# A gated decode layer on one core: first MLP layer as 16 wide products, first half of the output projection in whole 448-column rows, fewer and wider idle matmuls

## The chip, the cores and the metric

The kernel runs on one core of one Trainium2 chip. The metric is the device time of one execution in microseconds; the number for the kernel before is the median of five runs.

## The reference

One decode step of a layer with two branches, for a batch of 8 rows of width 448. Branch A is attention over a window of 1024 cached positions (16 query heads, 8 key/value heads, head size 256), followed by an output projection. Branch B is a two-layer MLP on the normalised input. A sigmoid gate g mixes the two.

```python
W = min(4096, max(256, Sk // 4))                 # 1024 of 4096 positions
q = (x @ wq).reshape(B, Sq, Hq, Dh)              # 8 x 1 x 16 x 256
k = jnp.repeat(k_cache[:, :, Sk - W:, :], 2, axis=1)
v = jnp.repeat(v_cache[:, :, Sk - W:, :], 2, axis=1)
p = softmax(einsum("bhqd,bhkd->bhqk", q, k) * Dh ** -0.5)
a = einsum("bhqk,bhkd->bhqd", p, v).reshape(B, Sq, 4096) @ wo      # 4096 x 448
h = gelu(layernorm(x) @ w1 + b1)                 # 448 x 1792, tanh form
b = h @ w2 + b2                                  # 1792 x 448
g = sigmoid((x * gate_w).sum(-1, keepdims=True))
return g * a + (1 - g) * b
```

## The kernel before

All large inputs pass once through a ring of nine slots of 2 MB each (`slots`, filled by `pump`). The order of the loads is written out by hand in `plan`: `wq` in two slots, the keys of step 0, `w1`, `w2`, then keys and values of the 16 steps in turn (values two steps behind the keys, `LAG`), and last `wo` in two slots. The first `wo` slot holds quarters 0 and 1 of the projection and comes as one transfer; the second holds quarters 2 and 3 and comes as three (quarter 2, six eighths of quarter 3, the last two eighths). SyncE's queue issues each load when `done()` has freed a slot. The order of work on each engine is the order in which the program writes it (`manual_schedule`).

A step u handles four key/value heads of one batch row. VectorE turns the keys in 32x32 blocks, in two halves (`turn_keys`, L350). TensorE multiplies them with the query weights `qw` (`scores`, L416 and L422; 8 products of 512 columns and a mask product for each half). Then come the maximum (`top`, `share`), the exponential on ScalarE (`expo`, L451), another turn on VectorE (`turn`, L464), its sum and inverse (`total`, `invert`), 16 products with the values (`values`, L494), a merge of two halves (L503, `gather` L509) and `finish` (L524, L527), which writes the scaled head outputs to `oT`. The main loop runs u = 1 to 15 and works off the parts of the steps before between the two halves of the scores.

Around the main loop:

- `norm_and_gate` and `query` prepare the normalised input `yT`, the gate `gg` and the query weights `qw`. GpSimd clears several tiles at the start.
- `mlp_hidden` (L540, L549) computes the first MLP layer transposed: 56 products whose stationary side is a 128x128 piece of `w1` and whose moving side is the 8 columns of `yT`. VectorE adds the bias and computes the GELU with ScalarE's Tanh. `mlp_out` (L585, L592) does the second layer in 14 products of 448 columns and one for the bias, and leaves the gated result in `mixb` (L594).
- `keep_clock` (L598) issues matmuls whose result nobody reads. They stand in the loop for u = 12, 13, 14 (six each) and at seven places of the tail.
- The tail, after the loop, finishes steps 14 and 15 and does the output projection. `begin` (L638) seeds two accumulators with `mixb` through an identity product: `A_lo` holds columns 0 to 223 in PSUM rows 0 to 7, `A_hi` columns 224 to 447 in rows 32 to 39. `spread_rows` (L651, L658) rearranges `oT` to `oP` by 16 small products and a VectorE copy, once for quarters 0 and 1 and once for quarters 2 and 3. `project(q)` (L667) then does eight pairs of 224-column products into the two accumulators. VectorE and ScalarE copy them to `res` (L709, L710), and one transfer stores it (L711).

Of the kernel before, what the change touches and what calls it, by code (L numbers as in the profile page):

```python
# [18 lines left out]
def kernel(  # L19
# [82 lines left out]
    def done(n=1):  # L102
        consumed[0] += n
        pump()
# [72 lines left out]
    def slot(*key):  # L177
        return slots[index[key]]

    consts.tile([P, 64], BF16, name="pad")  # L180
    x_sb = consts.tile([NB, D], BF16)
    eps_t = consts.tile([NB, 1], F32)
    rstd = consts.tile([NB, 1], F32)
# [24 lines left out]
    yz = consts.tile([NB, DT], BF16)  # L208
    nc.gpsimd.memset(xz[:], 0.0)
    xT = consts.tile([P, NX, NB], BF16)  # L210
    yT = consts.tile([P, NR + 1, NB], BF16)
    rowden = consts.tile([P, P], F32)
    sel2 = consts.tile([P, RQ], F32)
    own = consts.tile([P, PAIR], F32)
# [9 lines left out]
    each = consts.tile([NB, NB + P], F32)  # L224
    gg_s = consts.tile([P, NB], F32)
    ident_f = consts.tile([NB, NB], F32)
    ones_r = consts.tile([1, NB], BF16)
    mixb = consts.tile([NB, D], F32)
    res = consts.tile([NB, D], BF16)
    nc.gpsimd.tensor_copy(ident_f[:], ident[0:NB, 0:NB])  # L230
    nc.gpsimd.memset(ones_r[:], 1.0)

    def transposed(dst, src, srcz):
        tp = ps_misc.tile([P, NX, NB], BF16, tag="misc", name="tp")
# [56 lines left out]
    def norm_and_gate():  # L291
        stats = consts.tile([NB, nc.vector.BN_STATS_DIM], F32)
        nc.vector.bn_stats(stats[:], x_sb[:])
        mv = consts.tile([NB, nc.vector.BN_AGGR_DIM], F32)
        nc.vector.bn_aggr(mv[:], stats[:])
        nc.scalar.activation(rstd[:], mv[:, 1:2], ACT.Sqrt, bias=eps_t[:], scale=1.0)
        nc.vector.reciprocal(rstd[:], rstd[:])
        y_sb = consts.tile([NB, D], BF16)
        nc.vector.tensor_scalar(
            y_sb[:],  # L300
            x_sb[:],
            scalar1=mv[:, 0:1],
            scalar2=rstd[:],
            op0=ALU.subtract,
            op1=ALU.mult,
        )
        nc.vector.tensor_copy(
            yz[:].rearrange("p (b c r) -> p b c r", b=2, c=8),
            y_sb[:, DM:D].rearrange("p (b r c) -> p b c r", b=2, c=8),
        )  # L310
        tp = ps_misc.tile([P, NX, NB], BF16, tag="misc", name="tp")
        for r in range(NR):
            nc.tensor.transpose(tp[:, r, :], y_sb[:, r:DM:NR], ident[:NB, :NB])
        nc.tensor.transpose(tp[0:DT, NR, :], yz[:], ident[:NB, :NB])
        nc.vector.tensor_copy(yT[:, 0:NR, :], tp[:, 0:NR, :])
        nc.vector.tensor_copy(yT[0:DT, NR, :], tp[0:DT, NR, :])
        prod = consts.tile([NB, D], F32)
        gl = consts.tile([NB, 1], F32)
        nc.vector.scalar_tensor_tensor(
            prod[:],  # L320
            in0=x_sb[:],
            scalar=1.0,
            in1=gw_b[:],
            op0=ALU.mult,
            op1=ALU.mult,
            accum_out=gl[:],
        )
        gth = consts.tile([NB, 1], F32)
        nc.scalar.activation(gth[:], gl[:], ACT.Tanh, scale=0.5)
        nc.vector.tensor_scalar(  # L330
            gg[:, 0:1], gth[:], 0.5, 0.5, op0=ALU.mult, op1=ALU.add
        )
        nc.vector.tensor_scalar(
            gg[:, 1:2], gth[:], -0.5, 0.5, op0=ALU.mult, op1=ALU.add
        )
        nc.gpsimd.memset(each[:], 1.0)
        nc.vector.tensor_scalar_mul(each[:, 0:NB], ident[0:NB, 0:NB], gg[:, 0:1])
        gp = ps_misc.tile([P, NB], F32, tag="misc", name="gp")
        nc.tensor.matmul(  # L339
            gp[:], lhsT=each[:, NB : NB + P], rhs=each[:, 0:NB], start=True, stop=True  # L340
        )
        nc.vector.tensor_copy(gg_s[:], gp[:])
# [189 lines left out]
        )  # L532

    def mlp_hidden():
        hT = ps_misc.tile([P, NF, NB], F32, tag="misc", name="hT")
        w = slot("w1")
        for r in range(NR):
            o = r * F
            for c in range(NF):
                nc.tensor.matmul(  # L540
                    hT[:, c, :],
                    lhsT=w[:, o + c : o + F : NF],
                    rhs=yT[:, r, :],
                    start=(r == 0 and c == 0),
                    stop=False,
                    skip_group_check=True,
                )
        for c in range(NF):
            nc.tensor.matmul(  # L549
                hT[:, c, :],  # L550
                lhsT=w[0:DT, NR * F + c : (NR + 1) * F : NF],
                rhs=yT[0:DT, NR, :],
                start=False,
                stop=True,
                skip_group_check=True,
            )
        done()
        z = consts.tile([P, NF, NB], F32)
        nc.vector.tensor_tensor(
            z[:],  # L560
            hT[:],
            b1_sb[:].rearrange("p (c o) -> p c o", o=1).to_broadcast([P, NF, NB]),
            op=ALU.add,
        )
        z2 = consts.tile([P, NF, NB], F32)
        nc.vector.tensor_tensor(z2[:], z[:], z[:], op=ALU.mult)
        uu = z2
        nc.vector.tensor_scalar(
            uu[:], z2[:], 0.044715, 1.0, op0=ALU.mult, op1=ALU.add
        )  # L570
        w_ = consts.tile([P, NF, NB], F32)
        nc.vector.tensor_tensor(w_[:], uu[:], z[:], op=ALU.mult)
        th = consts.tile([P, NF, NB], F32)
        nc.scalar.activation(th[:], w_[:], ACT.Tanh, scale=0.7978845608028654)
        hh = th
        nc.vector.tensor_scalar(hh[:], th[:], 1.0, 0.5, op0=ALU.add, op1=ALU.mult)
        hs = consts.tile([P, NF, NB], BF16)
        nc.vector.tensor_tensor(hs[:], hh[:], z[:], op=ALU.mult)
        return hs

    def mlp_out(hs):
        bb = ps_misc.tile([NB, D], F32, tag="misc", name="bb")
        w = slot("w2")
        for c in range(NF):
            nc.tensor.matmul(  # L585
                bb[:],
                lhsT=hs[:, c, :],
                rhs=w[:, c * D : (c + 1) * D],
                start=(c == 0),
                stop=False,  # L590
            )
        nc.tensor.matmul(bb[:], lhsT=ones_r[:], rhs=b2_r[:], start=False, stop=True)  # L592
        done()
        nc.scalar.activation(mixb[:], bb[:], ACT.Copy, scale=gg[:, 1:2])  # L594

    def keep_clock(dst, n):
        for _ in range(n):
            nc.tensor.matmul(dst, lhsT=foreign[:], rhs=place[:], start=True, stop=True)  # L598

# [9 lines left out]
    for u in range(1, NQ):  # L609
# [14 lines left out]
            invert(u - LAG)  # L624
        scores(u, 1)
        if NQ - 4 <= u < NQ - 1:
            keep_clock(idle[:], 6)
        expo(u - 1)
    u = NQ - 1
    A_lo = ps_misc.tile([NB, DH2], F32, tag="misc", name="A_lo")  # L630
    A_hi = ps_s.tile([P, W], F32, tag="S", name="A_hi")
    halves = (A_lo[:], A_hi[32 : 32 + NB, 0:DH2])
    oP = consts.tile([P, NJ8, NHQ, NB], BF16)
    oTv = oT[:].rearrange("p (q i) j b -> p i j q b", i=HPQ)

    def begin():
        for i, dst in enumerate(halves):
            nc.tensor.matmul(  # L638
                dst,
                lhsT=ident_f[:],  # L640
                rhs=mixb[:, i * DH2 : (i + 1) * DH2],
                start=True,
                stop=False,
                skip_group_check=True,
            )

    def spread_rows(q0, q1):
        pp = ps_sm.tile([P, HPQ, NJ, q1 - q0, NB], F32, tag="sm", name="pp")
        for i in range(HPQ):
            for m in range(HPQ):  # L650
                nc.tensor.matmul(  # L651
                    pp[32 * i : 32 * i + 32, m],
                    lhsT=ident[:, m::HPQ],
                    rhs=oTv[:, i, :, q0:q1, :],
                    start=True,
                    stop=True,
                )
        nc.vector.tensor_copy(  # L658
            oP[:, :, q0:q1, :], pp[:].rearrange("p m j q b -> p (m j) q b")
        )  # L660

    def project(q):
        w = slot("wo", q - q % 2)
        for j in range(NJ8):
            o = ((q % 2) * NJ8 + j) * D
            for i, dst in enumerate(halves):
                nc.tensor.matmul(  # L667
                    dst,
                    lhsT=oP[:, j, q, :],
                    rhs=w[:, o + i * DH2 : o + (i + 1) * DH2],  # L670
                    start=False,
                    stop=(q == NHQ - 1 and j == NJ8 - 1),
                    skip_group_check=True,
                )
# [6 lines left out]
    values(u - 1)  # L681
    top(u)
    share(u)
    keep_clock(A_hi[:, W // 2 : W], 3)
    invert(u - 1)
    expo(u)
    gather(u - 1)
# [2 lines left out]
    turn(u)  # L690
    total(u)
    invert(u)
    spread_rows(0, HALF)
    keep_clock(A_hi[:, W // 2 : W], 4)
    values(u)
    gather(u)
    keep_clock(A_hi[:, W // 2 : W], 3)
    finish(u)
    keep_clock(A_hi[:, W // 2 : W], 3)
    spread_rows(HALF, NHQ)  # L700
    keep_clock(A_hi[:, W // 2 : W], 2)
    project(0)
    project(1)
    keep_clock(A_hi[:, W // 2 : W], 3)
    project(2)
    keep_clock(A_hi[:, W // 2 : W], 2)
    project(3)

    nc.vector.tensor_copy(res[:, 0:DH2], halves[0])  # L709
# [32 lines left out]
```

## Time and profile before

| | |
|---|---|
| five runs, us | 190.59 median, 190.40 to 190.74 |
| profiled execution: its own time, us | 190.59 |
| its span, first to last instruction, us | 188.5 |
| granted TensorE clock, mean | 0.955 |
| busy in the span: PE, PEld, DVE, ACT, POOL, us | 135.7, 67.2, 126.3, 45.4, 6.4 |
| instructions: PE, PEld, DVE, ACT, POOL | 940, 940, 177, 93, 14 |
| transfers | 77.83 MB in 6316 packets, 413 GB/s mean |
| instruction queue q8 | 7 packets, 0.11 MB |

The profile is of one execution. PE is TensorE's matmul row and PEld its weight loads, which overlap; DVE is VectorE, ACT ScalarE, POOL GpSimd, SP SyncE. All times in the views are counted from the start of the span. The ends of matmuls are modelled, their starts are recorded. A float32 product appears as two loads and two matmuls.

### The profile page before, as it was taken

The numbers are of one execution on the slowest core, as the hardware profiler recorded it, in microseconds if no ns is written. First come the engines' busy times: TensorE is split into PE (matmuls) and PEld (weight loads), VectorE is DVE, ScalarE is ACT, GpSimd is POOL, SyncE is SP. The second block draws the span as 40 slices with busy tenths as digits, with TensorE's granted clock in tenths as the row PEclk, the third lists the DMA queues.
The fourth block names the chain that finished last, engine by engine and source line by source line (L and its number), as shares of the span: only waits on it lengthen the run. The fifth ranks groups of instructions, "written<-read, shape, count | busy, mean of one in ns | idle before, by whom it ended". The sixth has DMA issues, their size and how long they took to land.

```text
span 188.5 us, 2342 instructions
## 1 busy us (share of the span) xinstructions
PE 135.7 (72%) x940; PEld 67.2 (36%) x940; DVE 126.3 (67%) x177; ACT 45.4 (24%) x93; POOL 6.4 (3%) x14
## 2 busy tenths in 40 slices
PE   0027938998867578666967599848398969698993
PEld 0012823344424233422433344323143424245451
DVE  2850378989969494949494949495868677685300
ACT  3032220133140404040404021404022404035200
POOL 8400000000000000000000000000000000000000
PEclk9999999999999969996999859999789999999999
DMA  6999999999999999999999999999999999999990
GB/s 210 406 438 425 441 420 433 435 424 431 435 431 421 431 442 431 421 428 438 438 422 428 435 435 421 431 435 442 424 424 431 438 431 424 428 438 425 407 398 21
DMA packets 6316, 77.83 MB, mean 413 GB/s; under 512 B 841, under 2 KB 994, under 8 KB 1698
## 3 DMA queue, kind: packets, MB, share of 16 engines
q1 hardware_dynamic: 6128, 77.67, 96.9%
q8 instruction: 7, 0.11, 0.2%
q10 hardware_dynamic: 178, 0.02, 0.1%
q14 instruction: 3, 0.02, 0.0%
HBM read 77.68 MB, written 0.01 MB: 412 GB/s over the span
## 4 chain that ended last, share of the span: by engine, by line
DMA 78%; DVE 9%; PE 8%; ACT 2%; issue 1%; DVEq 0%; ACTq 0%; SPq 0%
DMA slot<-in_A_k_cache_dram 59%; DMA slot<-in_A_wo_dram 17%; DVE kt L350 4%; PE S L422 2%; DMA x_sb<-in_A_x_dram 2%; PE Sq L364 2%; ACT qw L405 1%; DVE qw L407 1%; DVE xz L242 1%; PE qt L379 1%; ACT qs L374 1%; PE qp L392 1%; PE PO L494 1%; PE A_lo L667 0%; PE gp L339 0%
## 5 line engine op out<-in xcount | busy, mean ns | idle before, releaser
L350 DVE STREAM_TRANSPOSE kt<-slot 128x2048 int32<-128x2048 int32 x32 | 73.7, 2306 | 30.9 <-DMA slot<-in_A_k_cache_dram 30.8
L422 PE MATMUL S<-kt,qw 128*128 128x512 bf16 x256 | 67.6, 409 | 29.1 <-DVE kt L350 28.6
L422 PEld LDWEIGHTS <-qw 128*128 128x128 bf16 x256 | 26.0, 102 | 67.2 <-issue 44.3
L527 ACT ACTIVATE oT<-fin,gg_s 128x16 bf16<-128x16 f32 x16 | 5.2, 328 | 74.2 <-PE fin L524 74.2
L451 ACT ACTIVATE E<-S,nmx 128x1024 bf16<-128x1024 f32 x16 | 22.2, 1390 | 1.9 <-DVE nmx L448 1.8
L434 DVE TENSOR_REDUCE mx<-S 128x1 f32<-128x1024 f32 x16 | 19.0, 1185 | 0.0
L494 PE MATMUL PO<-slot,ET 128*16 128x512 bf16 x256 | 17.5, 395 | 0.3 <-DMA slot<-in_A_v_cache_dram 0.3
L503 ACT ACTIVATE first<-PO,own 128x256 f32<-128x256 f32 x16 | 7.6, 473 | 27.1 <-PE PO L494 25.8
L416 PE MATMUL S<-place,foreign 128*128 128x512 bf16 x32 | 12.7, 397 | 0.1
L464 DVE STREAM_TRANSPOSE ET<-E 128x512 int32<-128x512 int32 x16 | 11.2, 698 | 2.2 <-ACT E L451 2.2
L442 PE MATMUL mz<-m,same 128*128 128x4 f32 x32 | 6.2, 265 | 5.6 <-ACT oT L527 5.5
L442 PEld LDWEIGHTS mz<-m,same 128*128 128x128 f32 x32 | 5.0, 195 | 7.5 <-ACT oT L527 6.6
L475 PEld LDWEIGHTS den<-rowsum,rowden 128*128 128x128 f32 x32 | 6.4, 205 | 3.1 <-issue 0.8
L494 PEld LDWEIGHTS <-ET 128*16 128x16 bf16 x256 | 5.1, 89 | 5.0 <-issue 1.2
L416 PEld LDWEIGHTS <-foreign 128*128 128x128 bf16 x32 | 3.2, 100 | 8.7 <-issue 6.9
L598 PE MATMUL A_hi<-place,foreign 128*128 128x512 bf16 x20 | 5.5, 381 | 0.0
L407 DVE CAST qw<-qp 32x512 bf16<-32x512 f32 x4 | 2.7, 687 | 3.4 <-ACT qw L405 3.4
L486 ACT ACTIVATE rsel<-sel,rb 128x8 f32<-128x8 f32 x16 | 4.7, 292 | 1.0 <-DVE rb L485 1.0
L475 PE MATMUL den<-rowsum,rowden 128*128 128x1 f32 x32 | 4.9, 222 | 0.0
L598 PEld LDWEIGHTS <-foreign 128*128 128x128 bf16 x38 | 3.3, 101 | 3.7 <-issue 0.8
L598 PE MATMUL idle<-place,foreign 128*128 128x512 bf16 x18 | 4.4, 378 | 0.0
L289 POOL MEMSET qw<- 128x5120 bf16 x1 | 4.4, 4354 | 0.0
(144 smaller groups left out, 95.5 us busy)
## 6 DMA issues: line engine op xcount, KB each, us to landing
slot<-in_A_k_cache_dram SPq DMA_DIRECT2D x16, 2048.0 KB, 35.2
slot<-in_A_v_cache_dram SPq DMA_DIRECT2D x16, 2048.0 KB, 36.8
slot<-in_A_wq_dram SPq DMA_DIRECT2D x1, 2048.0 KB, 7.6
slot<-in_A_wo_dram SPq DMA_DIRECT2D x1, 1792.0 KB
slot<-in_B_w_dram SPq DMA_DIRECT2D x1, 1568.0 KB
slot<-in_B_w_dram SPq DMA_DIRECT2D x1, 1344.0 KB, 11.8
slot<-in_A_wq_dram SPq DMA_DIRECT2D x1, 1024.0 KB, 9.7
slot<-in_A_wo_dram SPq DMA_DIRECT2D x1, 896.0 KB, 33.6
```

Source lines behind the costliest of these rows:

```text
L350: nc.vector.transpose(kt[:].rearrange("p c k x r -> p (c k x r)").bitcast(WORD), kn[:, hf * CH * Dh : (hf + 1) * CH * Dh].bitcast(WORD),)
L416: nc.tensor.matmul(S[u][:, cols], lhsT=foreign[:], rhs=place[:], start=True, stop=False)
L422: nc.tensor.matmul(S[u][:, cols], lhsT=qw[:, j, u, m * RQ : m * RQ + P], rhs=kt[:, :, k, :, par], start=False, stop=(k == NK - 1 and par = ...
L434: nc.vector.reduce_max(mx[:], S[u][:], axis=AXIS.X)
L442: nc.tensor.matmul(mz[:], lhsT=same[:], rhs=m4[:], start=True, stop=True)
L451: nc.scalar.activation(E[:].rearrange("p c x i -> p c i x"), S.pop(u)[:].rearrange("p (c i x) -> p c i x", i=PAIR, x=BLK), ACT.Exp, bias=n ...
L464: nc.vector.transpose(ET[:].rearrange("p c r i -> p (c r i)").bitcast(WORD), E[:].rearrange("p c x i -> p (c x i)").bitcast(WORD),)
L475: nc.tensor.matmul(den[u][:], lhsT=rowden[:], rhs=rowsum[:], start=True, stop=True)
L494: nc.tensor.matmul(PO[32 * t : 32 * t + PAIR * RQ], lhsT=ET[:, c, 0:RQ, :], rhs=vn[:, PAIR * c * Dh : PAIR * (c + 1) * Dh], start=(c < QUA ...
L503: nc.scalar.activation(first[:], PO[:, 0, :], ACT.Copy, scale=own[:, 0:1])
L527: nc.scalar.activation(oT[:, half * RQ : (half + 1) * RQ, :, b].rearrange("p h j -> p j h"), sm[:], ACT.Copy, scale=gg_s[:, b : b + 1],)
L598: nc.tensor.matmul(dst, lhsT=foreign[:], rhs=place[:], start=True, stop=True)
```

## The change

Three things are changed.

The first MLP layer turns its sides round: `yT`, padded to 32 columns, is the stationary side and 448 columns of `w1` move, in four row pieces by four column groups, 16 products. The result stands in four 32-row groups of `hP`. ScalarE copies it to SBUF with its columns reordered (`hS`), and VectorE turns the 32x32 blocks (`hB`), which gives the layout that the bias and GELU steps had. These are regrouped: two of VectorE's small steps are folded into fused ones, and the factor 0.5 of the GELU moves into the gate (-0.25, 0.25) and the bias vector of the second layer (2.0 instead of 1.0). The tile `yT` is cleared by GpSimd at the start, and the padding tile `pad` grows by 64 bytes.

The idle products change: in the loop two narrow ones (512 columns, bf16) and one wide one (512 columns, float32, `same` against `qw` read as float32) instead of six narrow; in the tail one wide, one wide, one wide, two narrow and two narrow, instead of 3, 4, 3, 3, 2, 3 and 2 narrow. They write to the tile `spare`.

The output projection: one `spread_rows` for all four quarters, after `finish(u)`. Quarters 0 and 1 go as 16 products of 448 columns into one accumulator, `whole`, which `begin` has seeded. ScalarE saves it to `mixb` (`save_whole`), and after quarter 2, which starts fresh accumulators in the two halves, an identity product adds it to them (`add_whole`). Quarter 3 follows.

```diff
-    yT = consts.tile([P, NR + 1, NB], BF16)
+    yT = consts.tile([P, NR + 1, BLK], BF16)
+    nc.gpsimd.memset(yT[:], 0.0)
...
     def mlp_hidden():
-        hT = ps_misc.tile([P, NF, NB], F32, tag="misc", name="hT")
+        FT = F // QUAD
+        hP = ps_misc.tile([P, FT], F32, tag="misc", name="hP")
         w = slot("w1")
-        for r in range(NR):
-            o = r * F
-            for c in range(NF):
+        for r in range(NR + 1):
+            rows = P if r < NR else DT
+            for t in range(QUAD):
+                o = r * F + t * FT
                 nc.tensor.matmul(
-                    hT[:, c, :],
-                    lhsT=w[:, o + c : o + F : NF],
-                    rhs=yT[:, r, :],
+                    hP[BLK * t : BLK * (t + 1), :],
+                    lhsT=yT[0:rows, r, :],
+                    rhs=w[0:rows, o : o + FT],
...
         done()
+        hS_ = epool.tile([P, W], BF16, tag="E", name="hS")
+        hS = hS_[:, 0 : 2 * FT].bitcast(F32).rearrange("p (c x) -> p c x", x=BLK)
+        nc.scalar.copy(
+            hS.rearrange("p c x -> p x c"),
+            hP[:].rearrange("p (x c) -> p x c", c=NF),
+        )
+        hB_ = epool.tile([P, W], BF16, tag="ET", name="hB")
+        hB = hB_[:, 0 : 2 * FT].bitcast(F32).rearrange("p (c x) -> p c x", x=BLK)
+        nc.vector.transpose(
+            hB_[:, 0 : 2 * FT].bitcast(WORD),
+            hS_[:, 0 : 2 * FT].bitcast(WORD),
+        )
+        hT = hB[:, :, 0:NB]
...
-    def keep_clock(dst, n):
+    def keep_clock(dst, n, wide=0):
+        for _ in range(wide):
+            rhs = qw[:, 0].rearrange("p u a -> p (u a)")[:, 0:W].bitcast(F32)
+            nc.tensor.matmul(dst, lhsT=same[:], rhs=rhs, start=True, stop=True)
         for _ in range(n):
             nc.tensor.matmul(dst, lhsT=foreign[:], rhs=place[:], start=True, stop=True)
...
         if NQ - 4 <= u < NQ - 1:
-            keep_clock(idle[:], 6)
+            keep_clock(idle[:], 2, 1)
...
+    def project_whole(q):
+        w = slot("wo", q - q % 2)
+        for j in range(NJ8):
+            o = ((q % 2) * NJ8 + j) * D
+            nc.tensor.matmul(
+                whole,
+                lhsT=oP[:, j, q, :],
+                rhs=w[:, o : o + D],
+                start=False,
+                stop=False,
+                skip_group_check=True,
+            )
+
+    def save_whole():
+        nc.scalar.copy(mixb[:], whole)
+
+    def add_whole():
         for i, dst in enumerate(halves):
             nc.tensor.matmul(
                 dst,
                 lhsT=ident_f[:],
                 rhs=mixb[:, i * DH2 : (i + 1) * DH2],
-                start=True,
+                start=False,
...
     share(u)
-    keep_clock(A_hi[:, W // 2 : W], 3)
+    keep_clock(spare[:], 0, 1)
...
     invert(u)
-    spread_rows(0, HALF)
-    keep_clock(A_hi[:, W // 2 : W], 4)
+    keep_clock(spare[:], 0, 1)
     values(u)
     gather(u)
-    keep_clock(A_hi[:, W // 2 : W], 3)
+    keep_clock(spare[:], 0, 1)
     finish(u)
-    keep_clock(A_hi[:, W // 2 : W], 3)
-    spread_rows(HALF, NHQ)
-    keep_clock(A_hi[:, W // 2 : W], 2)
-    project(0)
-    project(1)
-    keep_clock(A_hi[:, W // 2 : W], 3)
+    keep_clock(spare[:], 2)
+    spread_rows()
+    keep_clock(spare[:], 2)
...
+    project_whole(0)
+    project_whole(1)
+    save_whole()
     project(2)
-    keep_clock(A_hi[:, W // 2 : W], 2)
+    add_whole()
     project(3)
```

## The prediction

> **What bounds the kernel now.** I read the transfer table first, then the chain of waits, then the timeline and the windows of the last microseconds. The page's DMA row stands at 9 from the second slice to the last but one, at 407 to 442 GB/s: the kernel streams 77.67 MB and computes beside it. The chain that ended last says the same, and its end shows where compute can still count.
>
> ```profile
> 74.18 38.84 DMA slot<-in_A_k_cache_dram
> ...
> 151.93 32.97 DMA slot<-in_A_wo_dram
> 184.91 0.04 issue
> 184.95 0.26 PE A_lo L667
> ...
> 185.88 0.05 PE A_hi L667
> 185.93 0.37 DVE res L709
> ```
>
> Columns: start, length, what. Until 184.91 the chain is slots waiting for transfers. Only what follows the landing at 184.91 is compute: `project(3)`, the copy of the result, the store. So a gain or loss reaches the time in one of two ways: the last quarter of `wo` lands at another moment, or `project(3)` starts later than that landing. I call its start S; it is 184.95 now. The windows show how the stream runs dry (us; busy time of PE, PEld, DVE, ACT, POOL; clock; DMA share; GB/s):
>
> ```profile
> 182.00:183.00 1.00, 1.00 (x11) 0.26 (x9) 0.00 (x0) 0.00 (x0) 0.00 (x0) 1.00 0.95 385
> 183.00:184.00 1.00, 1.00 (x18) 0.71 (x18) 0.00 (x0) 0.00 (x0) 0.00 (x0) 1.00 0.69 267
> 184.00:185.00 1.00, 0.48 (x4) 0.13 (x4) 0.00 (x0) 0.00 (x0) 0.00 (x0) 1.00 0.14 52
> ```
>
> A share of 0.14 means about two of 16 transfer engines still at work: the landing waits for stragglers. The queue table of the window 181.5 to 183.2 names a cause, and the page its total:
>
> ```profile
> q1 hardware_dynamic: 156, 0.65, 93.9%
> q8 instruction: 1, 0.02, 3.2%
> ...
> q8 instruction: 7, 0.11, 0.2%
> ```
>
> One of seven 16 KB instruction packets falls here; 3.2% of 16 engines over 1.7 us is 0.87 us on one engine. The landing records of the piece that `project(3)` waits for have the last three of 16 engines at 184.02, 184.29 and 184.91. Without that packet the piece would be in at about 184.29, 0.62 us earlier.
>
> **Instructions.** The instruction packets come near 25, 55, 83, 112, 141, 163 and 182 us, when 236, 505, 758, 994, 1256, 1476 and 1825 of TensorE's 1905 recorded instructions (loads, products and some 25 waits) had started: one packet for about 265. The change removes: first MLP layer 112 to 32 (-80); idle products in the loop 36 to 24 (-12; a float32 product counts four) and in the tail 40 to 20 (-20); spreading 64 to 32; `project(0)` and `(1)` 64 to 32; `begin` 8 to 4; it adds 8 for `add_whole`. Sum -172, so 1733 are left. The smallest count per packet so far is 246 (1476 over 6), so a seventh is due between instruction 1722 (7 x 246) and 1825; the last quarter's 32 are held back by their transfer, so some 1700 at most are reached by then. The packet drops out of the end, and the others come later (the sixth near 170 us). That is worth the 0.62 us only if TensorE is ready.
>
> The Trainium skill, "Runtime: NRT & Kernel Launch", section Instruction fetch mechanics, gives blocks of 256 instructions and calls the cost of crossing one "mostly hidden"; the trace agrees on the spacing, not on the hiding at the stream's end. By that rule the packet is worth 0.
>
> **First MLP layer: 0.** Before, 56 products run from 21.83 to 24.47, and TensorE then waits for `qw` (25.77) and `kt` (28.85). Sixteen 448-column products cost between 0.76 us (four column groups at once) and 3.0 (one by one, at the 0.189 of L585: 14 in 2.81, the last 0.35); both end before 25.77. The copy on ScalarE lies between L405 (512 columns, 0.58) and L374 (1024, 1.02) and ends before 27, where VectorE arrives at 31.0. VectorE gains a transpose (L464, 512 words: 0.70) and loses two steps (0.22 each): +0.2 to +0.3. It idles 30.9 us waiting for K, and slots are asked for 35 us before they land, so nothing follows; uncovered it would be that 0.3. The GpSimd memset of `yT` (0.19, as `foreign`) moves the `qw` memset's end from 6.74 to 6.93, needed at 21. SP's issues, the one behind `w1` at 24.50 among them, move by under 2 us against those 35.
>
> **Idle products.** Six narrow ones take 1.46 us with the last one's 0.38, so 0.216 apiece: 1.29. No wide float32 one is in the trace; from `begin` (224 columns, a pass at 174.26, the next at 174.45) 512 columns in two passes are 0.87, and 0.87 + 0.43 = 1.30. No change in occupancy. In the tail the three wide ones replace 3, 4 and 3 narrow ones, up to 0.22 longer each; they stand before waits of 0.2 (rsel, 173.69), 0.3 (V, 176.25) and 0.4 us (os, 178.46), so 0 to 0.1, taken as 0.
>
> **The tail up to S.** By the landing records V of the last step is in at 176.25 and the first half of `wo` at 180.54; the change leaves both. One full spread instead of the second half: it can start at 179.6, when `oT` is ready, instead of 179.75; its copy has 256 columns (L658, 128 columns: 0.29; L509, 256 columns: 0.44 to 0.48), so `oP` is ready near 180.55. No loss. Then:
> - whole rows: 16 x 0.189 = 3.02 from 180.58, to 183.60. The halves took half of that, 16 pairs x 0.095 = 1.52, the two running side by side.
> - `project(2)`: 8 pairs x 0.095 = 0.76, to 184.36. Its piece is in at 182.73.
> - meanwhile the save: the last whole row starts at 183.42; L592 to L594 shows 0.38 from such a start to ScalarE's, so 183.80; a 448-column copy costs 0.52 (on the line through L710, 224 columns 0.34, and L405, 512 columns 0.58) to 0.62 (L594). Ready for TensorE at 184.37 to 184.47, 0.05 after its end.
> - `add_whole`: the step from 128-row products to an 8-row one leaves a gap of 0.09 (L585's last start 36.56 + 0.19, L592 at 36.84) and the step back another 0.09 (36.84 + 0.19 to 37.12). So 184.45 + 2 x 0.19 + 0.09 = 184.92. If both gaps vanish the save sets it: 184.37 + 0.38 = 184.75; if save and gaps add up, 184.47 + 0.09 + 0.38 + 0.09 = 185.03.
>
> I take 184.92, as the L592 rows are the nearest case, with ends 184.75 and 185.1. As a check: before, TensorE was ready for the last quarter at 184.37; the idle products and gaps that go took 1.50 (182.11 to 182.97, 183.73 to 184.37), the whole rows add 1.50, the add and its gaps 0.56, so it is ready at 184.93. The landing gives 0.62 back and TensorE takes it: S moves by -0.03 (-0.2 to +0.15). After S nothing changes (188.5 - 184.95 = 3.55). The profiled execution took 190.59, exactly the median, around its span of 188.5: 190.59 - 0.03, about 190.55.
>
> **Rivals.** *The landing decides (faster).* If `project(3)` is ready at 184.33, S gains 0.62: 190.0. For it: the straggler is plain, and the modelled ends of products may hide slack. Against: it needs a chain 0.6 us shorter than its own rows, of which the 3.02 is firm. It decides if `add_whole` ends by 184.3. A smaller form: if a later sixth packet changes the order of the stragglers, V and `wo` land 0.3 earlier.
>
> *The clock falls (slower).* The clock of a 3.4 us stretch follows the work of the one before:
>
> ```profile
> 62.60:66.02 3.42, 1.25 (x6) 0.42 (x5) 1.59 (x1) 0.82 (x2) 0.00 (x0) 1.00 0.97 417
> 66.02:69.43 3.41, 2.63 (x7) 0.94 (x7) 3.37 (x6) 0.00 (x0) 0.00 (x0) 0.50 1.03 442
> 120.63:124.04 3.41, 1.51 (x7) 0.57 (x6) 1.26 (x1) 1.08 (x2) 0.00 (x0) 1.00 1.04 447
> 124.04:127.46 3.42, 2.31 (x14) 1.44 (x13) 3.38 (x6) 0.00 (x0) 0.00 (x0) 1.00 0.97 417
> 160.80:164.20 3.40, 1.64 (x8) 0.68 (x7) 2.52 (x2) 0.00 (x0) 0.00 (x0) 1.00 1.05 443
> ```
>
> After 1.25 us of products it fell to 0.50, after 1.51 it stayed. At 160.8 there are 1.64, mostly idle products. If a float32 product counts half, 0.43 drops out: 1.21, below the bound. Half the clock from 164.2 makes eight scores 3.2 to 3.4 us (66.80, 28.85) instead of 1.9, and the last values, covered by 0.86 (ET done 175.46, start 176.32), come 0.6 late: 191.2. A fall in the tail itself doubles the whole rows: +3.0, 193.6. Nothing shows float32 counting less; but the covers in the tail get thinner too. The Trainium skill, "TensorE: Matmul & The Clock Gate", asks for no idle gap over about 3 us; after 150 us no gap is that long, so by it nothing falls, where the rows ask for more than 1.25 us of work.
>
> *The handover is dearer (slower).* Save, add and gaps form a serial path that is new; at 1.0 for the copy (L374) S would be 185.3: 191.0. It decides from S above 185.33.
>
> **Numbers.** No movement that counts, 0.54, its own range 190.35 to 190.75. The landing decides, 0.18, at 190.0. The clock falls, 0.20, at 191.2 and up. A dearer handover, 0.08, at 191.0. About 0.2% (0.38 us) is what a measurement of this kernel can tell from none: faster 0.18, same 0.54, slower 0.28. The range runs from the landing's 190.0 to 191.4, leaving out half of the clock's case and the better end of the first rival.
>
> **What would show it.** Right: six instruction packets, none after 175; the last `wo` pieces in before 184.5; `project(3)` starting at 184.8 to 185.1 with `add_whole`, not a transfer, as what ended its wait; clock 1.00 from 138 us on. Wrong: S set by DMA, a clock of 0.50 after 150, or a seventh packet near the end.

## The result and the profile after

The changed kernel is slower by about a third of a per cent: 191.25 us in the median of 43 executions (190.28 to 193.10) against 190.71 in 79 of the kernel before, beside it on the same chip (190.36 to 193.29). The ratio is 1.0035 with a 95% interval of 1.0022 to 1.0049. The forecast was no movement, at 190.55; the result lies inside the range, in the part kept for the slower cases.

The profiled execution took 190.91 us with a span of 189.1 (before: 190.59 and 188.5). The chain that ended last (start, length, what):

```profile
142.14 39.01 DMA slot<-in_A_wo_dram
181.20 3.10 PE A_all L673 x16
184.30 0.18 PE A_lo L701
184.87 0.28 PE A_lo L701 x3
185.15 0.28 PE A_lo L687
185.44 0.18 PE A_lo L687
185.63 0.19 PE A_lo L701
...
186.53 0.37 DVE res L744
```

Before, the last transfer on this chain was the last quarter of `wo`, and only `project(3)`, the copies and the store came behind it. Now it is an earlier one, the first half of `wo`, in at 181.15. From there on TensorE alone carries the chain: the whole rows (L673), `project(2)` (L701), the addition (L687), `project(3)` (L701). The lengths in this view are partly modelled; by the recorded starts, `project(3)` begins at 185.57, which is 0.62 later than before (184.95). The windows say the same (busy time of PE, PEld, DVE, ACT, POOL; clock; DMA share; GB/s):

```profile
183.00:184.00 1.00, 1.00 (x9) 0.43 (x7) 0.00 (x0) 0.00 (x0) 0.00 (x0) 1.00 0.65 256
184.00:185.00 1.00, 1.00 (x18) 0.70 (x14) 0.00 (x0) 0.52 (x1) 0.00 (x0) 1.00 0.12 45
185.00:186.00 1.00, 1.00 (x16) 0.52 (x16) 0.00 (x0) 0.00 (x0) 0.00 (x0) 1.00 0.00 0
```

Before, TensorE was half idle from 184 to 185, waiting for the last bytes; now it has work throughout, and the transfers are over while it still computes. The transfers themselves have changed as well. The queue table of the window 172.5 to 173.6 and the page's total:

```profile
q1 hardware_dynamic: 27, 0.44, 96.8%
q8 instruction: 1, 0.02, 5.0%
...
q8 instruction: 6, 0.10, 0.2%
```

There are six instruction packets, the sixth at 172.56. The first piece of data that lands after it, V of the last step, is in at 176.90 (before: 176.25), and the first half of `wo` at 181.15 (before: 180.54). The last quarter lands where it did, at 184.88 (before: 184.91).

### The profile page after: what moved, and what is told of

Read it like the earlier page. It is cut to its first block, busy times and chain, and to the rows that moved or that the text cites. A ratio compares the mean times of both kernels' runs of the same rounds, so it can differ in the third digit from the quotient of the medians.

```text
span 189.1 us, 2171 instructions
## 1 busy us (share of the span) xinstructions
PE 132.9 (70%) x854; PEld 63.0 (33%) x854; DVE 126.9 (67%) x175; ACT 46.8 (25%) x95; POOL 6.5 (3%) x15
## 4 chain that ended last, share of the span: by engine, by line
DMA 81%; PE 10%; DVE 5%; ACT 1%; issue 1%; SPq 0%; DVEq 0%; ACTq 0%
DMA slot<-in_A_k_cache_dram 59%; DMA slot<-in_A_wo_dram 21%; PE S L423 2%; DMA x_sb<-in_A_x_dram 2%; PE Sq L365 2%; PE A_all L673 2%; DVE xz L243 1%; DVE kt L351 1%; PE PO L495 1%; PE A_lo L701 1%; ACT qs L375 1%; PE fin L525 0%; PE qp L393 0%; PE qt L380 0%; PE mz L443 0%
## 5 line engine op out<-in xcount | busy, mean ns | idle before, releaser
L417 PEld LDWEIGHTS <-foreign 128*128 128x128 bf16 x32 | 3.2, 100 | 8.8 <-issue 7.1
L449 DVE TENSOR_REDUCE nmx<-mz 128x1 f32<-128x4 f32 x16 | 2.3, 144 | 3.4 <-PE mz L443 3.2
L437 DVE TENSOR_SCALAR m<-block,mx 128x4 f32<-128x4 f32 x16 | 3.7, 229 | 0.6
```

The source lines that it names most:

```text
L417: nc.tensor.matmul(S[u][:, cols], lhsT=foreign[:], rhs=place[:], start=True, stop=False)
```

## Experiments

### Is it the same in other executions?

The changed text again in three more runs, the kernel before again in one; no edit.

> The changed kernel once more, for a second trace. Theory 1 (packet): one of the six instruction packets falls on a transfer engine that was not early, some time before the last values or the first half of wo are in; these land about 0.6 us late and project(3) starts about 4.36 us after the first half of wo. Then the sum 'wo first half lands, plus 4.4' holds again, whatever the landing is, and the landing may differ between executions (181.15 in the first trace, 180.54 in the kernel before). Theory 2 (clock): the granted clock falls after 150 us and the chain from the first half of wo to project(3) is longer than 4.4. Time: 191.2 by both.

> The kernel before once more, for a second trace. Theory A (no slack): packets push an engine back in this kernel too, so here as well the first half of wo may be in at 181.2 and the last quarter at 184.9, and the pairs still fit in between: project(3) starts with the landing, 184.3 to 185.0. Theory B (the change moved a packet onto a worse engine): the first half of wo is in at 180.5 again. Time 190.7 by both.

> The changed kernel for a third trace. Executions at 190.9 (full clock) and 191.7 (half clock from 175.3 to 178.7) are known. Lateness: first half of wo at 181.1-181.3, last product 5.08 us behind it if the clock is full, 190.9-191.1; half clock in 173-180 adds 0.8: 191.7. An execution below 190.7 should have the first half of wo in before 180.8.

> The changed kernel once more, beside e17_seventh_packet on the same chip: median 191.1-191.4, two to four of twelve executions with over 2.4 us outside the span; in the trace the first half of wo at 181.1-181.3 and the last product 5.08 us behind it.

The changed kernel: 191.33 (12 executions, ratio 1.0030, 0.9997 to 1.0063), 191.04 (one), 191.15 (12, ratio 1.0028, 1.0002 to 1.0054). The kernel before again: 190.70 (12, ratio to itself 1.0025, 1.0001 to 1.0049). So identical texts can come out 0.25% apart in twelve executions; smaller differences below are read together with the traces. In the two traces of before the first half of `wo` is in at 180.54 and 180.44, which is the sign of e5's theory B; in the four of the changed kernel it is in at 181.15, 181.27, 181.29 and 181.63. Whether the change makes it late is taken up below.

### Which part is it?

The projection and the idle products of the tail as before, the rest changed (e2); the MLP as before, the rest changed (e3); the idle products narrow, in the old number where one wide had replaced three, four or six (e4); the new tail alone on the kernel before (e7).

```diff
 e2, against the changed kernel
-    project_whole(0)
-    project_whole(1)
-    save_whole()
+    project(0)
+    project(1)
+    keep_clock(A_hi[:, W // 2 : W], 3)
     project(2)
-    add_whole()
+    keep_clock(A_hi[:, W // 2 : W], 2)
...
 e4, against the changed kernel
-            keep_clock(idle[:], 2, 1)
+            keep_clock(idle[:], 6)
-    keep_clock(spare[:], 0, 1)
+    keep_clock(spare[:], 3)
```

> Undoes the output projection and the idle products of the tail (pairs of 224 columns, two spreads, as before), keeps the new MLP layer and the loop's wide idle products; 1814 TensorE instructions. Theory 1: even if the first half of wo lands late, the chain behind it is 1.8 us shorter, so project(3) starts with the last landing, 184.9 or earlier: 190.5 to 190.7. Theory 3 (the MLP layer or the loop's idle products cost the time, by the clock): stays at 191.1 to 191.3.

> Undoes the first MLP layer only (56 products as before), so 80 instructions come back ahead of step 1 and every later packet comes about 80 instructions, 9 us, earlier: the sixth near 163. Theory 1: the delay stays if the engine that the packet falls on is the same (lag is kept to the end): 191.2; it goes if the engine changes with the moment: 190.6. Theory 3: 190.6 if the MLP layer were to blame.

> Undoes the kind of the idle products only: narrow bf16 ones at the same places (6 in the loop, 3, 4, 3, 2, 2 in the tail), 1754 instructions. Theory 1: no change, 191.2 (20 instructions move a packet by 2 us). Theory 2: if the wide float32 products keep the clock up less well, the long executions of 192 and more vanish: 190.9 median and a clock of 1.0 after 150 us.

> The kernel before with the new tail alone (whole rows, save, add, one spread, the tail's new idle products); MLP layer and loop as before; 1827 instructions. Theory A: the first half of wo plus 4.4 us sets project(3): 191.2, as the whole change. Theory B: with the packets near their old places about 190.6 to 190.8.

Measured: e2 190.51 (ratio 0.9993, 0.9977 to 1.0009), e3 191.08 (1.0012, 0.9983 to 1.0041), e4 191.14 (1.0012, 0.9980 to 1.0044), e7 191.05 (1.0031, 1.0017 to 1.0044). Taking the projection and the tail's idle products back removes the loss (e2, with the new MLP layer), and putting in the new tail alone brings it (e7, with the old one). So the tail is the cause, and the MLP layer is not needed for it. e3 and e4 add little: their intervals hold both no change and the whole loss, and e4's slow executions did not vanish (192.13 and 192.15). How the tail costs time, the traces of these runs did not say. The profiled execution of e7 was its fastest, at 190.52, with `project(3)` level with the landing; that of e2 was its slowest, at 191.42, and is read under "The clock".

### A late transfer or a low clock?

The text of e7 four times more.

> The text of e7_tail_alone once more: its profiled execution (190.52) was the fastest of its twelve, whose median was 191.05, so its trace doesn't show what costs the median 0.4. Theory: in a usual execution the last values or the first half of wo come late, by a packet on a late engine (V after 176.6, full clock) or by the half clock between 173 and 179; project(3) then starts 4.3 us behind the first half of wo or later, at 185.4-185.9, with TensorE as its releaser. Rival: project(3) is at 185.1 as in the first trace and the loss lies behind it, in the last copies or the output's transfer.

> The new tail alone, a further trace. Its two traces so far are of executions at 190.5, where project(3) starts level with the landing of the last quarter; the usual execution is at 191.0. Theory (lateness): in an execution above 190.8 the first half of wo is in 0.5 later than 180.5-180.7, at 181.0-181.3, the clock is full to the end, and the last product starts 5.07 us behind that landing. Rival (clock): the first half of wo is in by 180.7 and a stretch at half clock lies between 173 and 180. Below 190.7 the trace says nothing.

> As e13_tail_alone_3: above 190.8 either the first half of wo at 181.0-181.3 with the last product 5.07 us behind it (lateness), or half clock between 173 and 180 (clock).

> As e13_tail_alone_3: above 190.8 either the first half of wo at 181.0-181.3 with the last product 5.07 us behind it (lateness), or half clock between 173 and 180 (clock).

e12 gave 190.94 (12 executions, ratio 1.0009, 0.9990 to 1.0027), with a profiled one of 190.50; its interval holds no change, where that of e7, the same text, does not. e13, e14 and e15 gave 191.11, 190.93 and 190.87. Chains of e12 and then e13, the same text:

```profile
142.38 38.27 DMA slot<-in_A_wo_dram
180.70 3.10 PE A_all L667 x16
...
186.03 0.37 DVE res L738
```

```profile
142.17 39.12 DMA slot<-in_A_wo_dram
181.33 3.10 PE A_all L667 x16
...
186.67 0.37 DVE res L738
```

The same 3.10, and the same 5.33 or 5.34 from the whole rows to the copy; only the landing of the first half of `wo` differs, 180.66 against 181.29, and the end moves with it, 0.64. The clock is 1.00 from 143 us to the end of the work in e13, e14 and e15. This is lateness and not the clock. By starts, all in us:

| trace | its time | first half of `wo` in | last product starts | between |
|---|---|---|---|---|
| e17 (below) | 190.25 | 180.49 | 185.57 | 5.08 |
| e12, tail alone | 190.50 | 180.66 | 185.73 | 5.07 |
| e15, tail alone | 190.87 | 181.04 | 186.12 | 5.08 |
| e14, tail alone | 190.93 | 181.11 | 186.19 | 5.08 |
| the changed kernel | 190.91 | 181.15 | 186.23 | 5.08 |
| e13, tail alone | 191.11 | 181.29 | 186.37 | 5.08 |
| e16, changed | 191.04 | 181.29 | 186.36 | 5.07 |
| e18, changed | 191.40 | 181.63 | 186.71 | 5.08 |
| before | 190.59 | 180.54 | 185.63 | waits for the last quarter |
| e11, pairs (below) | 190.32 | 181.20 | 185.65 | waits for the last quarter |

With whole rows the end follows the first half of `wo` one to one. e3 fits too (181.22, 186.30, 5.08). The other traces with the whole new tail have something later to wait for: in e7 it is the last quarter, and e1, e4 and e8 are read under "The clock".

The same text can have that landing early or late. In the late traces the landing records show one of 16 transfer engines 1.3 to 1.8 us behind the median; in nine of the 14 it falls behind when the sixth instruction packet comes, in the others earlier, and it stays there to the end. In e7 and e13 the packet comes at the same moment (162.52 and 162.40), yet V of the last step is in at 176.16 in the one and at 177.04 in the other. In the first, the latest engine stays 0.7 behind the median; in the second, it goes from 0.63 to 1.53.

The packet records show which packet does it. Most packets last 0.92 to 0.98 us (those that come when the stream runs dry up to 1.29), but up to two of an execution last 0.88 or 0.89, and it is after these that the latest engine falls back: before, from 0.85 to 1.37 at the seventh packet (182.00); in the changed kernel, from 0.53 to 1.37 at the sixth (172.56). The place of the first of them differs between executions of one text: seventh in e7 and e12, sixth in e13, e14 and e15. What makes these packets different is not shown. e17 and e4 have none, and no engine falls back. Only e9 is late without one; its latest engine was 1.6 behind already at 60 us.

Of the 20 traces of all versions, 14 have the first half of `wo` in after 181.0 and six before 180.7. At full clock the span of a kernel with the new tail is that landing plus 7.97 us, so executions without a trace tell it as well: spans of 188.8 or less, an early landing, are 6 of 44 for the changed kernel and 4 of 27 for the tail alone. The shares are alike, although the sixth packet of the tail alone comes at the time of before. Whether the kernel before lands late as often is not shown: its two traces are early, and its pairs would hide a late landing from its time.

### Is it the length of the chain?

The changed kernel with quarters 0 and 1 in pairs again (e6, repeated as e11), without the save and the addition (e9), and with whole rows for quarter 0 only (e10).

```diff
 e6
-    project_whole(0)
-    project_whole(1)
-    save_whole()
+    project(0)
+    project(1)
     project(2)
-    add_whole()
 e9
-    save_whole()
     project(2)
-    add_whole()
 e10
     project_whole(0)
-    project_whole(1)
     save_whole()
-    project(2)
+    project(1)
     add_whole()
+    project(2)
```

> The changed kernel with quarters 0 and 1 in pairs of 224 columns again, no save and no add; the one spread, the idle products (none between the quarters) and the new MLP layer stay; 1762 instructions. Theory A: from the first half of wo to ready it takes 16 + 8 pairs, 2.3 us, so project(3) starts with the last landing: 190.4 to 190.7. Theory B: no change against the changed kernel beyond the chain, 190.5 to 190.9. If the idle products or the one spread cost the time: 191.1 or more.

> The changed kernel without the save of the whole rows and without the addition that takes them over: quarters 0 and 1 are still multiplied as whole rows, but their sum and the MLP are left out of the output. Theory (a serial chain without slack from the first half of wo to project(3)): the chain shrinks from 4.36 to 0.05 + 3.02 + 0.09 + 0.76 = 3.92 us; with the first half of wo in at 181.15 project(3) starts at 185.1 and not 185.56, so the median falls by about 0.45 to 190.7-190.9. Rival (the wide rows themselves, or the later V, cost the time, however the rows are taken over): the median stays at 191.1-191.4.

> Half the dose: quarter 0 in whole rows, saved while quarter 1 is done in pairs, then the addition, project(2) and project(3); all is computed. Theory: from the first half of wo to project(3) 0.05 + 8 x 0.189 + 0.09 + 0.76 + 0.09 + 0.38 + 0.09 + 0.76 = 3.73 us; from 181.15 that is 184.88, level with the landing of the last quarter (184.88): project(3) at 184.9-185.0, median 190.5-190.7. Rival (whatever is wrong comes with the save and the addition as such, not with the length): as the changed kernel, 191.1-191.4.

> The text of e6_pairs once more, for a second trace and a second interval. Theory: the landing of the last quarter sets project(3) whatever the first half of wo does, 184.9-185.0 in the trace; median 190.3-190.6, ratio to before 0.998-1.000, none or one execution in twelve above 191.5. Rival (the first reading was luck): 190.7 or more.

| version | from the first half's landing to the last product, us | median, us | ratio to before |
|---|---|---|---|
| changed (first, e1, e18) | 5.08 (e1: 5.78, at half clock) | 191.25, 191.33, 191.15 | 1.0035, 1.0030, 1.0028 |
| e10 | 4.48 | 190.68 | 0.9995 (0.9973 to 1.0017) |
| e9 | 4.51 | 190.44 | 0.9992 (0.9968 to 1.0015) |
| e6 | 4.44 | 190.41 | 0.9990 (0.9979 to 1.0000) |
| e11 | 4.45 | 190.31 | 0.9974 (0.9953 to 0.9996) |

Each of the four traces had the first half of `wo` as late as the changed kernel, at 181.06 to 181.28, and the last quarter in at 184.82 to 185.05. A chain that leaves the last product within about 4.5 us of the first half is covered by the last quarter's landing. The whole rows with their handover are 0.6 longer than that, and all of it shows. e9 came out below what was expected (190.7 to 190.9), because its chain to `project(3)` took 3.84 us and not 3.92, and so was level with the landing. That neither e9 nor e10 can be told from before, while both intervals (up to 1.0017 and 1.0015) end below the changed kernel's (from 1.0022), settles two rivals. "The wide rows themselves" falls with e9, which has all of them; "the save and the addition as such" falls with e10, which has both. The end of the chain in e11:

```profile
151.79 33.14 DMA slot<-in_A_wo_dram
184.97 0.26 PE A_lo L674
185.95 0.37 DVE res L712
```

It is the picture of before, with the last quarter deciding, although the first half of `wo` is in 0.66 later than before. e6 and e11 are also the best version found: none of their 24 executions is above 190.71. Since they keep the tail's wide idle products and the one spread, these are not what costs the time either.

### The clock

Two more narrow idle products behind `begin`.

> The changed kernel with two narrow idle products more behind begin, where TensorE waits for the exponential: 0.43 us more work in the stretch from 172 to 175. Theory C (part of the cost is the clock that falls at 175 in some executions, as in the second trace): the executions over 191.7 get rarer, median 190.9 to 191.1. Theory A alone: 191.2.

e8 was slower still: 191.79 (6 executions, ratio 1.0065, 1.0045 to 1.0084). Its clock never fell after 134 us, but the last values started 0.48 us after their V was in (177.59 after 177.11), where the changed kernel lost 0.04: the filler now ends after what it was to bridge. Its last product starts 5.37 us behind the first half of `wo`. Yet the clock does fall just ahead of the tail in some executions. e1's profiled one took 191.73 with the first half of `wo` at 181.27:

```profile
171.88:175.29 3.41, 3.25 (x21) 1.56 (x14) 1.68 (x6) 2.32 (x5) 0.00 (x0) 1.00 0.96 403
175.29:178.70 3.41, 3.40 (x18) 0.69 (x18) 0.17 (x1) 0.30 (x1) 0.00 (x0) 0.50 1.00 422
```

At half clock the last values cost 1.86 us and not 1.04, the whole rows start at 182.02, and the last product at 187.05: 0.70 later than the landing by itself would have it. e4's trace shows the same from 175.17 to 178.58; of the 15 traces with the new tail or part of it these are the only two with half clock there. In the changed kernel such a delay goes to the end in full. It is the second way in which the chain costs time; how often it comes can't be read from the executions without a trace.

The pairs do not cover every delay either. In e2's trace (191.42) the clock is 0.50 from 155.88 to 162.70, after a stretch in which products were busy for 0.82 us. The last values start at 177.95, 1.00 us after their V, and `project(3)` at 185.97, although the last quarter is in at 184.95. That execution is the only one of e2's twelve above 190.74.

### The executions at the upper end

17 of the changed kernel's 43 executions are above 191.5, and 9 of 79 of before. About half of the changed kernel's 17 have a long span, the others a usual span and 2.4 to 3.4 us outside it, where 1.8 is usual. Spans of 190 us and more stand in no trace (the longest is e1's, 189.95) and come in before too (e5: 190.1 and 190.8), so their cause is open. e17 adds 16 small products early on, so that the seventh instruction packet comes at 183.70, during the last quarter's wait, and not behind the end.

```diff
+        if 3 <= u < 7:
+            for _ in range(4):
+                nc.tensor.matmul(
+                    idle[:, 0:8], lhsT=foreign[:], rhs=foreign[:, 0:8], start=True, stop=True
+                )
```

> The changed kernel with 16 more products of 8 columns (4 each in the steps u = 3 to 6, nobody reads them): 32 TensorE instructions more, as many in all as the version with pairs has, within 4. In the executions listed for the changed kernel, a quarter have 2.4 to 3.4 us outside the span of the profile where 1.8 is usual; of the versions with pairs and of the tail alone none has. Theory: with 1733 instructions the seventh instruction packet comes behind the end and the end of the program waits for it; with 32 more it comes at about 184, during the last quarter, so no execution has more than 2.3 us outside its span, and the median falls by 0.1-0.3 to 190.9-191.1, the 0.35-0.45 of the serial chain staying. Rival (it has nothing to do with the packet): as many executions with over 2.4 us outside the span as in the changed kernel beside it, and its median.

e17: 190.96 (ratio 1.0014, 0.9993 to 1.0036), at most 1.89 us outside the span. e18, beside it on the same chip: 191.15, at most 2.24, and so without the executions that were to be compared. This pair leaves it open. Over all runs the association is strong: in versions whose trace has no seventh packet before 186 us, 18 of 111 executions have more than 2.4 us outside the span; in those with one at 181.8 to 184.4, 1 of 99. That the packet is waited for is likely, but not shown.

## Why the prediction was wrong

**The step that failed** is the first sentence on the tail: V in at 176.25, the first half of `wo` at 180.54, and "the change leaves both". These were values of one execution. In the texts with the new tail the landing of the first half varies between executions by more than a microsecond (180.22 to 181.63 in their traces), and the usual value is near 181.15. In the kernel before, pairs leave slack there, and e6 and e11 show that pairs cover a landing at 181.1 to 181.2; in the changed kernel the lateness goes to the end. In the profiled execution of the changed kernel the chain therefore started 0.61 later than the prediction took it to. The prediction had computed TensorE ready at 184.93 against a landing at 184.91, hence no slack at all, and gave S +0.15 at the upper end. With 181.15 in its own sum S is 185.5; measured were 185.57. No chance stood on that: the rivals moved the clock, the last landing and the handover, and where one of them moved the landing that starts the chain, it was by 0.3 to the early side.

**The length of the chain was right.** Predicted 4.34 us from the first whole row to `project(3)` (180.58 to 184.92), measured 4.37 (181.20 to 185.57). The save, too: predicted 0.38 behind the last whole row and 0.52 long; it starts 0.39 behind it (184.03 to 184.42).

```profile
184.42 0.52 ACT L683 COPY mixb<-A_all 8x448 f32<-8x448 f32 x1 [4.28 <-PE A_all L673]
```

So the rival of a dearer handover falls: the handover cost what its rows said.

**The instruction packets** were right in number and roughly in place: six up to the end of the stream, the sixth at 172.56 for "near 170". The consequence was half right. The last quarter should have landed at 184.29 without the late packet; it is near that where no engine has fallen behind by then (184.25 in e17, 184.44 in e12, 183.97 in e4), but in the usual execution the sixth packet leaves a straggler of its own, and the landing is 184.88. The rival in which the landing decides came true in none of these: in e17, with both landings early, `project(3)` starts at 184.90 and not at 184.25, because its chain takes 4.41 us from the first half of `wo` (180.49). Its time of 190.25 is below that of before by 0.06 inside the span and 0.28 outside it. The Trainium skill, "Runtime: NRT & Kernel Launch", section Instruction fetch mechanics, calls the crossing of a block "mostly hidden". In this saturated stream it is not always so: one packet is 0.88 to 0.97 us on one engine, and in the late traces one engine's data are 1.3 to 1.8 us behind the median for the rest of the kernel.

**The MLP** was right at 0, by e2 and e7 together; e3 alone can't tell. Its 16 products took 1.09 us (bounds 0.76 to 3.0), ScalarE's copy 0.91 (bounds 0.58 to 1.02) and VectorE's turn 0.60 (0.70 taken), all long before the next wait ends:

```profile
20.38 1.09 PE L543 MATMUL hP<-slot,yT 128*32 128x448 bf16 x16
...
25.12 0.91 ACT L554 COPY hS<-hP 128x448 f32<-128x448 f32 x1
...
30.29 0.60 DVE L560 STREAM_TRANSPOSE hB<-hS 128x448 int32<-128x448 int32 x1
```

**The idle products** were right at 0, by e6 and e11, and the reason of the clock's rival was wrong. Products are busy for 1.64 us in the stretch in question, as before, and the next stretch keeps its clock. Had the wide float32 product counted half, 1.21 would be left, less than the 1.25 after which the clock fell; so it counts in full:

```profile
161.02:164.43 3.41, 1.64 (x7) 0.58 (x6) 2.99 (x3) 0.00 (x0) 0.00 (x0) 1.00 1.00 428
164.43:167.84 3.41, 2.99 (x30) 1.83 (x28) 3.37 (x4) 0.33 (x1) 0.00 (x0) 1.00 1.02 437
```

The clock did fall later, ahead of the last values, in e1 and e4. That is the rival's effect with another cause, since e4 has no wide products.

**Behind S** nothing was to change. Inside the span that holds: from the last product's start to the end of the span it is 2.89 us before and after. Outside the span it does not: 2.08 in the profiled execution before, 1.78 after. The 0.62 of S less this 0.30 is the 0.32 between 190.59 and 190.91. The medians lie 0.54 apart; the upper end of the executions adds to that, with the half clock as one cause that traces show, and how much each cause adds was not settled.

## What to carry to other kernels

A landing time from one trace is a sample. Where a change puts a serial chain behind a transfer, set the chain's length against the spread of that landing over several traces; a sum that leaves no slack is a forecast of "slower", since lateness adds and earliness is lost in the next wait. Fewer and wider products lose where pairs of narrow ones run side by side: here a 448-column row cost 0.189 us and a pair of 224 columns 0.095, and the difference took the slack out of the only stretch that still had some.

## What the runs showed of the hardware

- An instruction packet hits a transfer engine that the text of the program does not fix: the same text with its packet at the same time had V of the last step in at 176.16 or 177.04. In this saturated stream the lag stays until the stream ends: in the changed kernel the latest engine is 0.53 behind the median at 171.13, 1.37 at 176.90 and 1.28 at 184.88.
- The clock of a 3.41 us stretch follows what TensorE streamed in the stretch before, and not the busy time of the view, much of which can be latency: in e1 it fell after 3.25 us of busy products. Count 512 columns as 0.217 us (the spacing of the scores' products) and a float32 pass as twice that, count overlapping products once, and leave out products of 8 rows. Then in the kernel before 1.28 us from 103.56 were followed by half clock, and 1.30 from 120.63 by full clock. In all 20 traces up to 1.28 was followed by half clock and 1.29 or more by full clock, with one exception (e5, 1.32 from 113.20, fell). e1's stretch from 171.88 has 1.27, or 2.03 with `begin`'s 8-row products, and fell; e4's from 171.76 has 0.84, or 1.60. The way of counting was fitted to these traces and not tested by a run of its own. The Trainium skill, "TensorE: Matmul & The Clock Gate", Part 1, speaks of an activity window whose phase differs from run to run; the traces agree: the same text has such a boundary at 175.29 in e1 and at 174.67 in the first trace, and only the former fell.
- The time outside the span goes with the number of TensorE's instructions in most versions: medians of 1.96 to 2.07 us at 1905 (before), 1.88 to 1.91 at 1814 to 1827 (e2, e3, e7, e12), 1.79 to 1.83 at 1762 and 1766 (e6, e11, e17). At 1733 it is 1.80 to 1.93 (the changed kernel, e1, e18), where the executions of the upper end raise it. What takes it was not looked for; it is about all of the 0.3 us by which the profiled executions of e6 and e11 (190.22 and 190.32) run ahead of that of before (190.59), their last product starting at 185.56 and 185.65 where that of before starts at 185.63.
